# A spectral layer rebuilt as packed real transforms, and a dense layer with one Mish pass

## The chip, the core and the metric

The kernel runs on one core of one Trainium2 chip. The metric is the time that the device takes for one execution, in microseconds (us): 1333.09, the median of three runs between 1329.69 and 1336.48.

## The reference

A sequence of 2048 rows of 1024 bf16 numbers passes through four layers: spectral, dense, spectral, dense. Each normalizes its input and adds its result to that input. Both spectral layers have the same filter, both dense layers the same weights.

```python
def _A_ref(x, w_r, w_i):                      # spectral
    B, S, D = x.shape                         # 1, 2048, 1024
    X = jnp.fft.rfft2(x.astype(jnp.float32), axes=(-2, -1))
    X = X * (w_r + 1j * w_i)                  # (2048, 513)
    return jnp.fft.irfft2(X, s=(S, D), axes=(-2, -1)).astype(jnp.bfloat16)

def _B_ref(x, w1, b1, w2):                    # dense, F = 3584
    h = jnp.einsum("bsd,df->bsf", x, w1) + b1
    sp = jnp.log1p(jnp.exp(-jnp.abs(h))) + jnp.where(h > 0, h, jnp.zeros_like(h))
    act = h * jnp.tanh(sp)                    # Mish
    return jnp.einsum("bsf,fd->bsd", act, w2)

x = x + _A_ref(_layernorm(x), A_w_r, A_w_i)
x = x + _B_ref(_layernorm(x), B_w1, B_b1, B_w2)
x = x + _A_ref(_layernorm(x), A_w_r, A_w_i)
x = x + _B_ref(_layernorm(x), B_w1, B_b1, B_w2)
```

## The kernel before

The program has no scheduler: Python code adds instructions to one list per engine (`Prog`), and each list runs in the order in which it was written. `Res` objects remember who wrote and read a buffer last, and `Prog.add` turns that into semaphore waits. So an instruction waits in its engine's queue until its own data are there, and everything behind it on that engine waits too. All DMAs are issued from SyncE's queue (SP, line 247, the noncontiguous one line 246). The residual stream XS (2048 x 1024, bf16) stays in SBUF all the time as 16 tiles of 128 rows; the rest of SBUF is one arena, cut anew in every layer.

`gen_prologue` loads x in four DMAs and takes statistics of the 16 tiles, most of them on VectorE (`tile_stats`), six on ScalarE. `ln_finish` makes scales and offsets for all 16 tiles at once; it needs the statistics of all of them, so a layer starts when the one before has ended.

`gen_layer_A` is the two-dimensional transform as matrix products, one stage after the other over the whole sequence: normalize and transpose (L698), the 1024-point transform along a row as a dense product with the table MD (L722), transposes (L753), 16-point transforms along the sequence (L785, L787), 128-point transforms for each of 16 residues k2 (L819 to L831), the product with the filter on VectorE (L859 to L868), the inverse 128-point transforms (L889 to L901), transposes, inverse 16-point transforms (L934, L936), transposes (L994) and the inverse row transform as a dense product with M5 (L1026), added to XS (L1037). Everything stays in SBUF. MD, M5, the twiddle tables and the filter are loaded in each of the two spectral layers. Evictions from PSUM go through `copy_fn` (L284 on ScalarE, L285 on VectorE).

`gen_layer_B` works on four chunks of 512 rows. `gen_prep` normalizes a chunk (L566) and transposes it (L1196). `gen_mm1` computes h of a chunk, two tiles of 128 features at a time, in 28 groups of 16 matmuls over 8 tiles of the contraction (L1234), with W1 streamed in 28 pieces of 256 columns, hence 14 groups per chunk and 56 loads per layer. VectorE adds the bias (L1240); `emit_act_batch` passes over three groups at a time with Exp (L1127), Ln (L1151) and Tanh (L1158), with table loads between them; `emit_dve_finals` multiplies on GpSimd (L1171). `gen_mm2` multiplies by W2, which is resident (L1275), and adds to XS (L1286). The products of chunk c+1 stand before the output products of chunk c on TensorE.

## Time and profile before

| what | value |
|---|---|
| runs | 1333.09 us median, 1329.69 to 1336.48 |
| profiled execution, span from first to last instruction | 1334.5 us |
| TensorE | 1223.7 us busy, 92% of the span |
| VectorE, ScalarE, GpSimd | 44%, 50%, 18% busy |
| chain that ended last | TensorE 86%, VectorE 7%, ScalarE 4%, DMA 3% |
| read from HBM | 101.31 MB |

The profile has one execution, and its span is its own time; it lies between the runs. A busy share is an average over stages of different kind, and TensorE's busy time counts pipelined matmuls from issue to their modelled end. What a stage costs is read from the windows of that stage, and what a matmul costs in a run of many from the length of the run. A group of instructions shows the mean time of one and how long its engine was idle ahead of it.

### The profile page before, as it was taken

Reading aid. Unit: us, or ns where it says so; the run is one execution under the profiler, and the core shown is the slowest. Engines: PE = TensorE matmul, PEld = TensorE weight load, DVE = VectorE, ACT = ScalarE, POOL = GpSimd, SP = SyncE. Lnnn points to the kernel's source line nnn. Section 1 sums busy time; section 2 is a strip of 40 time slices with the busy share of each in tenths; the row PEclk is TensorE's granted clock in tenths of the full one; section 3 lists DMA queues with packets and bytes.
Section 4 is the critical chain, followed back from the end, with each engine's and each line's share of the span. In section 5 each row is a group of like instructions: output and inputs, shape, how many; then the busy total and the mean of one; then the engine's idle time right before and its main releaser. Section 6 shows DMA issues by size and latency. Waiting matters only on the chain.

```text
span 1334.5 us, 17411 instructions
## 1 busy us (share of the span) xinstructions
PE 1223.7 (92%) x7184; PEld 661.2 (50%) x7184; DVE 591.8 (44%) x1123; ACT 668.6 (50%) x1049; POOL 235.7 (18%) x116
## 2 busy tenths in 40 slices
...
GB/s 268 74 1 40 104 2 1 171 211 123 128 78 10 121 91 0 146 28 0 0 214 1 1 106 38 1 1 292 147 97 153 21 32 158 32 48 189 17 24 24
DMA packets 142958, 106.62 MB, mean 80 GB/s; under 512 B 7200, under 2 KB 130592, under 8 KB 141856
## 3 DMA queue, kind: packets, MB, share of 16 engines
...
q14 instruction: 21, 0.17, 0.0%
HBM read 101.31 MB, written 4.19 MB: 79 GB/s over the span
## 4 chain that ended last, share of the span: by engine, by line
PE 86%; DVE 7%; ACT 4%; DMA 3%; issue 1%; SPq 0%; DVEq 0%
PE PS L1275 29%; PE PS L1234 28%; PE PS L722 8%; PE PS L1026 8%; PE PS L753 2%; DMA ARENA<-in_B_w_dram 2%; DVE ARENA L566 2%; ACT ARENA L284 2%; PE PS L1196 2%; DVE BNST L490 1%; ACT ARENA L569 1%; PE PS L934 1%; PE PS L936 1%; PE PS L787 1%; PE PS L785 1%; DVE ARENA L862 1%
## 5 line engine op out<-in xcount | busy, mean ns | idle before, releaser
L1171 POOL TENSOR_TENSOR ARENA<-ARENA 128x1024 bf16<-128x1024 bf16 x112 | 235.5, 2130 | 1017.1 <-ACT ARENA L1158 1007.5
L1234 PE MATMUL PS<-ARENA 128*128 128x512 bf16 x1792 | 393.6, 382 | 6.0 <-DMA ARENA<-in_B_w_dram 4.4
L1275 PE MATMUL PS<-ARENA 128*128 128x512 bf16 x1792 | 387.8, 379 | 0.0
L1234 PEld LDWEIGHTS PS<-ARENA 128*128 128x128 bf16 x1792 | 176.2, 99 | 219.8 <-issue 11.2
L1275 PEld LDWEIGHTS PS<-ARENA 128*128 128x128 bf16 x1792 | 175.4, 98 | 211.4
L1240 DVE TENSOR_SCALAR ARENA<-PS,B 128x512 bf16<-128x512 f32 x224 | 168.1, 750 | 227.2 <-PE PS L1234 216.7
L1127 ACT ACTIVATE ARENA<-ARENA 128x1024 bf16<-128x1024 bf16 x112 | 112.1, 1044 | 245.3 <-DVE ARENA L1240 245.3
L284 ACT ACTIVATE ARENA<-PS 128x264 bf16<-128x264 f32 (+6 forms) x448 | 152.5, 432 | 118.3 <-PE PS L722 101.0
L1286 DVE TENSOR_TENSOR XS<-PS,XS 128x512 bf16<-128x512 f32 x64 | 44.2, 691 | 322.3 <-PE PS L1275 322.3
L285 DVE CAST ARENA<-PS 128x128 bf16<-128x128 f32 (+3 forms) x244 | 77.8, 365 | 89.3 <-PE PS L722 83.6
L722 PE MATMUL PS<-ARENA 128*128 128x352 bf16 (+1 forms) x768 | 113.2, 310 | 0.0
L1026 PE MATMUL PS<-ARENA 128*128 128x512 bf16 x512 | 110.9, 379 | 0.6 <-DVE ARENA L285 0.6
L1158 ACT ACTIVATE ARENA<-ARENA 128x1024 bf16<-128x1024 bf16 x112 | 110.4, 1046 | 0.4
L1151 ACT ACTIVATE ARENA<-ARENA 128x1024 bf16<-128x1024 bf16 x112 | 110.4, 1046 | 0.4
L285 DVE COPY ARENA<-PS 128x1024 bf16<-128x1024 bf16 (+2 forms) x152 | 78.5, 549 | 49.5 <-PE PS L753 29.5
L548 ACT ACTIVATE STAT<-STAT,EPS 128x16 f32<-128x16 f32 x4 | 1.2, 308 | 196.9 <-DVE STAT L536 194.8
L722 PEld LDWEIGHTS PS<-ARENA 128*128 128x128 bf16 x768 | 75.1, 98 | 37.5
L1026 PEld LDWEIGHTS PS<-ARENA 128*128 128x128 bf16 x512 | 49.9, 98 | 60.9 <-DVE ARENA L285 1.0
L490 DVE BATCH_NORM_STATS2 BNST<-XS 128x6 f32<-128x512 bf16 x116 | 74.2, 681 | 10.5 <-DMA XS<-in_A_x_dram 8.8
L1196 PE MATMUL PS<-IDENT,ARENA 128*128 128x128 bf16 x256 | 28.1, 308 | 39.4 <-DVE ARENA L566 39.4
L698 PE MATMUL PS<-IDENT,ARENA 128*128 128x128 bf16 x256 | 21.9, 250 | 36.2 <-ACT ARENA L569 35.3
L1037 DVE TENSOR_TENSOR XS<-PS,XS 128x512 bf16<-128x512 f32 x64 | 42.6, 665 | 25.6 <-PE PS L1026 25.6
...
## 6 DMA issues: line engine op xcount, KB each, us to landing
ARENA<-in_B_w_dram SPq DMA_DIRECT2D x112, 512.0 KB, 3.8
...
ARENA<-in_A_w_r_dram SPq DMA_DIRECT2D x32, 128.2 KB, 2.5
ARENA<-in_A_w_i_dram SPq DMA_DIRECT2D x32, 128.2 KB, 3.0
...
out_dram<-XS SPq DMA_DIRECT2D x16, 256.0 KB, 3.0
```

What stands on the lines that cost most here:

```text
L284: return lambda e: e.activation(out_ap, in_ap, ACT.Copy)
L285: return lambda e: e.tensor_copy(out_ap, in_ap)
L490: lt = dve.add(lambda e, n2=n2, j=j, lo=lo, hi=hi: e.bn_stats(BNST[:, n2, j, :], XS[:, n2, lo:hi]), waits=w)
L722: e.matmul(PS[:, bank, 0:n], XT[:, db, n2 * P:(n2 + 1) * P], MD[:, db, cs:ce], start=(db == 0), stop=(db == ND - 1)))
L1026: e.matmul(PS[:, bank, 0:n], JT[:, blk, n2 * P:(n2 + 1) * P], M5[:, blk, ds_:de_], start=(blk == 0), stop=(blk == ND - 1)))
L1127: it["tE"] = act.add(lambda e, st=st: e.activation(TMP[st][:, :], HB[st][:, :], ACT.Exp), waits=rT.wait_w() + res_HB[st].wait_r())
L1151: it["tS"] = act.add(lambda e, st=st: e.activation(TMP[st][:, :], TMP[st][:, :], ACT.Ln, bias=1.0, scale=1.0), waits=[(act, it["tE"])])
L1158: it["tT"] = act.add(lambda e, st=st: e.activation(TMP[st][:, :], TMP[st][:, :], ACT.Tanh), waits=[(act, it["tS"])])
L1171: tF = fin.add(lambda e, st=st, dst=dst: e.tensor_tensor(dst, HB[st][:, :], TMP[st][:, :], ALU.mult), waits=w)
L1234: e.matmul(PS[:, bank, 0:SCH], W1B[wslot][:, db, fl * P:(fl + 1) * P], XT[:, db, :], start=(db == 0), stop=(db == ND - 1)))
L1240: e.tensor_scalar(HB[st][:, fl * SCH:(fl + 1) * SCH], PS[:, bank, 0:SCH], B1[:, ft:ft + 1], None, op0=ALU.add),
L1275: e.matmul(PS[:, bank, 0:n], AT[:, ft, j * P:(j + 1) * P], W2[:, ft, ds_:de_], start=(ft == 0), stop=(ft == NF - 1)))
```

## The change

The file is rewritten. Queues, waits and the resident XS stay as they were in kind; the arrangement of rows changes, so that tile j holds rows 128 n2 + 8 j + q (n2 from 0 to 15, q from 0 to 7).

The spectral layer. Each tile is normalized (`ln`, on [128, 1] columns, inverse root by Newton steps on VectorE), written to DRAM (`xn_store`) and read back in another order (`xr_load`), 128 numbers of 256 bytes at a time; both are issued by GpSimd. One product per tile with the 128x128 table M (`s1`) does a 16-point transform along the sequence and an 8-point transform along the row at once, and keeps one real member of each conjugate pair. The 16 residues are then paired in 8 groups; for each group `s2` does the 128-point transforms along the row, `s3` those along the sequence and the filter, `i1` and `i2` the inverses. The groups are pipelined in 12 steps: s2 of group g, s3 of g-1, i1 of g-3, i2 of g-4. In the first spectral layer `filter_bins` also reorders the filter's rows (products with an exchange matrix, copies on GpSimd) and stores the result in DRAM, from where the second reads it. 128 transposes and one product per tile with the transposed table (`i4`) end the inverse; each tile goes to DRAM in 256-byte pieces and comes back in the order of XS (`a_add`), where VectorE adds it and takes statistics and LayerNorm for the dense layer.

The dense layer. The first product of two chunks runs group by group, so that a piece of W1 serves both; a single Mish activation with the bias goes from PSUM to the product's operand. The second half of the sequence is added and normalized between the output products of the first half. In the first dense layer each finished tile is normalized and stored for the next spectral layer, and `s1` of that layer runs between the last output products.

On VectorE, at the start of the program, before:

```order
L268 UNCONDITIONAL_BRANCH [waits barrier_Pool_Activation_PE_DVE_SP_release]
L490 BN_STATS BNST<-XS 128x6 [waits ds_x1]
L490 BN_STATS BNST<-XS 128x6
L492 BN_AGGR STAT<-BNST 128x2 [waits sem_DVE]
L490 BN_STATS BNST<-XS 128x6 x2
```

and now (b1 is the bias of the dense layer, x0 the first tile of x):

```order
L297 UNCONDITIONAL_BRANCH [waits barrier_Pool_Activation_PE_DVE_SP_release]
L375 CAST B1<-B1h 128x28 [waits b1]
L403 BN_STATS ST<-XS 128x6 [waits x0]
L404 BN_STATS ST<-XS 128x6
L405 BN_AGGR ST<-ST 128x2 [waits sem_DVE]
```

The conversion of the bias, which stood in the first dense layer, now stands ahead of the first statistics.

On TensorE, at the start of the first dense layer, before (L1026 ends the spectral layer, L1196 are transposes, L1234 the first product):

```order
L1026 MATMUL PS<-ARENA 128x512 [waits sem_DVE]
L1026 MATMUL PS<-ARENA 128x512 x7
L268 UNCONDITIONAL_BRANCH
L1196 MATMUL PS<-IDENT,ARENA 128x128 [waits sem_DVE]
L1196 MATMUL PS<-IDENT,ARENA 128x128 x31
L1234 MATMUL PS<-ARENA 128x512 [waits ds_w1b0,sem_DVE]
L1234 MATMUL PS<-ARENA 128x512 x15
```

and now, the last of 16 tiles of i4 (L750), transposes of tiles (L793) and the first product (L811):

```order
L750 MATMUL PS<-ARENA,MT 128x512
L793 MATMUL PS<-IDENT,ARENA 128x128 [waits sem_DVE]
L793 MATMUL PS<-IDENT,ARENA 128x128 x7
L793 MATMUL PS<-IDENT,ARENA 128x128 [waits sem_DVE]
L793 MATMUL PS<-IDENT,ARENA 128x128 x7
L793 MATMUL PS<-IDENT,ARENA 128x128 [waits sem_ACT,sem_DVE]
L793 MATMUL PS<-IDENT,ARENA 128x128 x7
L793 MATMUL PS<-IDENT,ARENA 128x128 [waits sem_ACT,sem_DVE]
L793 MATMUL PS<-IDENT,ARENA 128x128 x7
L793 MATMUL PS<-IDENT,ARENA 128x128 [waits sem_ACT,sem_DVE]
L793 MATMUL PS<-IDENT,ARENA 128x128 x7
L811 MATMUL PS<-ARENA 128x512 [waits w1_0,sem_ACT]
```

All 16 tiles of the inverse stand ahead of the first transposes, and the transposes of the second chunk's tiles stand among the first products.

On GpSimd, in the first dense layer, before (its first compute instructions, products of h and the gate):

```order
L1334 MEMSET const-uint8-127 128x1
L268 UNCONDITIONAL_BRANCH [waits barrier_Pool_Activation_PE_DVE_SP_gather]
L1171 ISA
L1171 TENSOR_TENSOR ARENA<-ARENA 128x1024 [waits sem_ACT,sem_DVE]
L1171 TENSOR_TENSOR ARENA<-ARENA 128x1024 [waits sem_ACT] x2
```

and now, among its output products (y_scratch holds the spectral layer's result, xn_scratch the next layer's normalized tiles):

```order
L246 DMA ARENA<-y_scratch 128x1x1024 [waits sem_DVE] x2
L246 DMA xn_scratch<-ARENA 16x8x1024 [waits sem_DVE]
L246 DMA ARENA<-y_scratch 128x1x1024
L246 DMA xn_scratch<-ARENA 16x8x1024 [waits sem_DVE]
L246 DMA ARENA<-y_scratch 128x1x1024
```

Loads of y and stores of the next layer's tiles alternate there. On TensorE at the same place, before:

```order
L1275 MATMUL PS<-ARENA 128x512 [waits ds_w2]
L1275 MATMUL PS<-ARENA 128x512 x83
L1275 MATMUL PS<-ARENA 128x512 [waits sem_DVE]
L1275 MATMUL PS<-ARENA 128x512 x27
L1275 MATMUL PS<-ARENA 128x512 [waits sem_DVE]
```

and now, an output group of 28 products (L828) and the transposes of a later tile (L793) in turn:

```order
L828 MATMUL PS<-ARENA 128x512 [waits w2_2,w2_3,w2_1,w2_0]
L828 MATMUL PS<-ARENA 128x512 x27
L793 MATMUL PS<-IDENT,ARENA 128x128 [waits sem_DVE]
L793 MATMUL PS<-IDENT,ARENA 128x128 x7
L828 MATMUL PS<-ARENA 128x512 x56
L793 MATMUL PS<-IDENT,ARENA 128x128 [waits sem_DVE]
```

Where the output products of a chunk stood alone, eight transposes of a tile that VectorE has normalized now stand after every second group.

The core of the new code:

```diff
+    def prologue(self):
+        sp, dve = self.sp, self.dve
+        xv = self.x[0].rearrange("(n2 j q) d -> j n2 q d", n2=16, j=16)
+        for j in range(16):
+            self.dma(sp, self.XS[:, j, :], xv[j], f"x{j}", writes=[self.r_xs[j]])
...
+        r = Res("b1h")
+        self.dma(sp, self.B1h[:], self.b1.rearrange("(f p) -> p f", p=P), "b1", writes=[r], noncontig=True)
+        self.op(dve, lambda e: e.tensor_copy(self.B1[:], self.B1h[:]), reads=[r], writes=[self.r_b1])
...
+    def ln(self, j):
+        dve = self.dve
+        st, rs = self.ST[:, j, :], self.r_st[j]
+        def on(fn):
+            self.op(dve, fn, reads=[rs], writes=[rs])
+        h, a, r, ri = st[:, 16:17], st[:, 17:18], st[:, 14:15], st[:, 14:15].bitcast(dt.int32)
+        on(lambda e: e.tensor_scalar(h, st[:, 13:14], 0.5, 0.5e-5, op0=ALU.mult, op1=ALU.add))
+        on(lambda e: e.tensor_scalar(ri, h.bitcast(dt.int32), -0.5, float(0x5f3759df - (1 << 22)), op0=ALU.mult, op1=ALU.add))
+        for _ in range(2):
+            on(lambda e: e.scalar_tensor_tensor(a, r, h, r, ALU.mult, ALU.mult))
+            on(lambda e: e.scalar_tensor_tensor(r, a, 1.5, r, ALU.subtract, ALU.mult))
+        on(lambda e: e.scalar_tensor_tensor(st[:, 15:16], st[:, 12:13], -1.0, r, ALU.mult, ALU.mult))
+        b = self.xn_buf[self.xn_n % 3]
+        self.op(dve, lambda e: e.tensor_scalar(b.ap, self.XS[:, j, :], st[:, 14:15], st[:, 15:16], op0=ALU.mult, op1=ALU.add),
+                reads=[self.r_xs[j], rs], writes=[b.res])
+        return b
...
+    def xn_store(self, j, b):
+        self.dma(self.pool, self.xn_d[j].rearrange("q n d -> n q d"), b.ap, f"xw{j % 3}", reads=[b.res],
+                 writes=[self.r_xnd[j]])
+    def xr_load(self, j):
+        k = self.xr_n % 4
+        xr = self.xr_buf[k]
+        self.dma(self.pool, xr.ap, self.xn_d[j].rearrange("q n (h l) -> (n h) q l", l=P), f"xr{k}",
+                 reads=[self.r_xnd[j]], writes=[xr.res])
+        return xr
...
+    def s1(self, j, xr):
+        ps, banks, _ = self.pair()
+        M = self.M
+        fns = []
+        for q in range(8):
+            fns.append(lambda e, q=q: e.matmul(ps[:, q * P:(q + 1) * P], xr.ap[:, q, :], M[:], start=True, stop=True))
+        self.group(fns, reads=[xr.res, self.r_m], writes=banks)
+        src = ps.rearrange("p (q k) -> p k q", q=8)
+        dst = self.Y.ap[:, :, 8 * j:8 * j + 8]
+        if j % 2:
+            self.op(self.act, lambda e: e.activation(dst, src, ACT.Copy), reads=banks, writes=[self.r_y[j]])
+        else:
+            self.op(self.dve, lambda e: e.tensor_copy(dst, src), reads=banks, writes=[self.r_y[j]])
...
+            for j in range(16 + 3):
+                if j < 16:
+                    if j % 2:
+                        self.stats_act(j)
+                    else:
+                        self.stats_dve(j)
+                    self.xn_store(j, self.ln(j))
+                    xr[j] = self.xr_load(j)
+                if j >= 3:
+                    self.s1(j - 3, xr[j - 3])
...
+                for c in range(2):
+                    self.op(pool, lambda e, d3=d3, lo=lo, c=c: e.tensor_copy(d3[:, c, :, 0:64], lo[:, c, 0:3, :]),
+                            reads=[wr[i].res], parts=[wt.res])
+                for kd, c0 in ((0, 7), (1, 3)):
+                    dd = wt.ap[:, :, 384 + 64 * kd:448 + 64 * kd]
+                    self.op(pool, lambda e, dd=dd, lo=lo, c0=c0: e.tensor_copy(dd, lo[:, :, c0, :]),
+                            reads=[wr[i].res], parts=[wt.res])
+                for c in range(2):
+                    src = ps[:, 512 * i + 192 * c:512 * i + 192 * c + 192].rearrange("p (k i) -> p k i", i=64)
+                    self.op(act, lambda e, d3=d3, src=src, c=c: e.activation(d3[:, c, :, 64:128], src, ACT.Copy),
+                            reads=banks, parts=[wt.res])
+                self.dma(sp, self.w_d[s], wt.ap, f"ws{n}", reads=[wt.res], writes=[self.r_wd[s]])
...
+        def s3(g, i):
+            ps, banks, _ = self.pair()
...
+            fns = [
+                lambda e: e.matmul(ps[:, 0:512], t[:, 0:128], z.ap[:, 0, :], start=True, stop=False),
+                lambda e: e.matmul(ps[:, 512:1024], t[:, 0:128], z.ap[:, 1, :], start=True, stop=False),
+                lambda e: e.matmul(ps[:, 512:1024], t[:, 128:256], z.ap[:, 0, :], start=False, stop=True),
+                lambda e: e.matmul(ps[:, 0:512], t[:, 256:384], z.ap[:, 1, :], start=False, stop=True),
+            ]
+            self.group(fns, reads=[z.res, ft.res], writes=banks)
+            x = X[(2 * g + i) % 4]
...
+            wt, yk = WT[(2 * g + i) % 4], YK[(2 * g + i) % 6]
+            ta, tb = T[2 * i], T[2 * i + 1]
+            self.op(dve, lambda e: e.tensor_tensor(ta.ap, x.ap, wt.ap[:, 0:1, :].to_broadcast([P, 2, 512]), ALU.mult),
+                    reads=[x.res, wt.res], writes=[ta.res])
+            self.op(dve, lambda e: e.tensor_tensor(tb.ap, x.ap, wt.ap[:, 1:2, :].to_broadcast([P, 2, 512]), ALU.mult),
+                    reads=[x.res, wt.res], writes=[tb.res])
+            yk.res.begin()
+            self.op(dve, lambda e: e.tensor_tensor(yk.ap[:, 0, :], ta.ap[:, 0, :], tb.ap[:, 1, :], ALU.subtract),
+                    reads=[ta.res, tb.res], parts=[yk.res])
+            self.op(dve, lambda e: e.tensor_tensor(yk.ap[:, 1, :], tb.ap[:, 0, :], ta.ap[:, 1, :], ALU.add),
+                    reads=[ta.res, tb.res], parts=[yk.res])
...
+        for step in range(8 + 4):
+            g2, g3, g4, g5 = step, step - 1, step - 3, step - 4
...
+            for h in range(2):
+                if 0 <= g2 < 8:
+                    s2(g2, h)
+                if 0 <= g2 < 8 and h == 0 and li == 0:
+                    filter_bins(g2)
+                if 0 <= g3 < 8:
+                    s3(g3, h)
+                if 0 <= g4 < 8:
+                    i1(g4, h)
+                if 0 <= g5 < 8:
+                    i2(g5, h)
+            if 0 <= g3 < 8 and g3 + 2 < 8:
+                load_tabs(g3 + 2)
+                load_w(g3 + 2)
+            if 0 <= g4 < 8 and g4 + 2 < 8:
+                load_btabs(g4 + 2)
...
+            for l in range(16):
+                fns.append(lambda e, l=l, m=m, pb=pb: e.transpose(pb[:, l * P:(l + 1) * P], Uall[:, :, 16 * m + l], self.IDENT[:]))
+            self.group(fns, reads=r_u + [self.r_ident], writes=banks)
...
+    def i4(self, j):
...
+        fns = []
+        for h in range(2):
+            fns.append(lambda e, h=h: e.matmul(ps[:, h * 512:(h + 1) * 512], self.MT[:],
+                                               UT.ap[:, 64 * h:64 * h + 64, 8 * j:8 * j + 8], start=True, stop=True))
+        self.group(fns, reads=r_ut + [self.r_mt], writes=banks)
+        sg = self.sg_buf[j % 3]
+        src = ps.rearrange("p (l q) -> p q l", q=8)
+        self.op(self.act, lambda e: e.activation(sg.ap, src, ACT.Copy), reads=banks, writes=[sg.res])
+        self.dma(self.sp, self.y_d[j].rearrange("q n (h l) -> (n h) q l", l=P), sg.ap, f"yw{j % 3}",
+                 reads=[sg.res], writes=[self.r_yd[j]])
+    def a_add(self, j):
+        yt = self.yt_buf[j % 3]
+        self.dma(self.pool, yt.ap, self.y_d[j].rearrange("q n d -> n q d"), f"yr{j % 3}", reads=[self.r_yd[j]], writes=[yt.res])
+        self.op(self.dve, lambda e: e.tensor_tensor(self.XS[:, j, :], self.XS[:, j, :], yt.ap, ALU.add),
+                reads=[yt.res], writes=[self.r_xs[j]])
+        self.stats_dve(j)
+        return self.ln(j)
...
+        def mm1(c, fg):
+            n = base + 14 * (c // 2) + fg
+            wb = self.w1_buf[n % 4]
...
+                at, ra = AT[c % 2], r_at[c % 2][ft]
+                self.op(act, lambda e, bank=bank, ft=ft: e.activation(at.ap[:, ft, :], PS[:, bank, :], ACT.Mish,
+                                                                      bias=self.B1[:, ft:ft + 1]),
+                        reads=[self.r_bank[bank], self.r_b1], writes=[ra])
+            if c % 2 and self.w1_next == n + 4 and n + 4 < base + 28:
+                self.load_w1()
...
+            xs = self.XS[:, j, h * 512:(h + 1) * 512]
+            self.op(dve, lambda e: e.tensor_tensor(xs, PS[:, bank, :], xs, ALU.add),
+                    reads=[self.r_bank[bank]], writes=[self.r_xs[j]])
+            if h == 0:
+                return
+            if last:
+                ov = self.out[0].rearrange("(n2 j q) d -> j n2 q d", n2=16, j=16)
+                self.dma(sp, ov[j], self.XS[:, j, :], "st", reads=[self.r_xs[j]])
+            else:
+                self.stats_dve(j)
+                self.xn_store(j, self.ln(j))
...
+        for j in range(16):
+            self.i4(j)
+        xn = {}
+        for j in range(4):
+            xn[j] = self.a_add(j)
+            if j:
+                transposed(0, j - 1, xn[j - 1], act)
+        transposed(0, 3, xn[3], act)
...
+        for j in range(4, 8):
+            xn[j] = self.a_add(j)
+            if j == 5:
+                mm1(0, 0)
+            elif j == 7:
+                mm1(0, 1)
+            transposed(1, j - 4, xn[j])
+        W2, r_w2 = load_w2()
+        for fg in range(14):
+            if fg + 2 < 14:
+                mm1(0, fg + 2)
+            mm1(1, fg)
+        for t in range(8):
+            xn[8 + t] = self.a_add(8 + t)
+            mm2(t // 4, t % 4, 0)
+            transposed(2 + t // 4, t % 4, xn[8 + t])
+            mm2(t // 4, t % 4, 1)
+        for fg in range(14):
+            mm1(2, fg)
+            mm1(3, fg)
+        for t in range(4):
+            mm2(2, t, 0)
+            mm2(2, t, 1)
+        if not last:
+            self.begin_A()
+            xr = {j: self.xr_load(j) for j in range(4)}
+        j = 0
+        for t in range(4):
+            for h in range(2):
+                mm2(3, t, h)
+                for _ in range(2 if not last and t else 0):
+                    self.s1(j, xr[j])
+                    if j + 4 < 12:
+                        xr[j + 4] = self.xr_load(j + 4)
+                    j += 1
+                if not last and h:
+                    xr[12 + t] = None
+        if not last:
+            while j < 16:
+                if xr.get(j) is None:
+                    xr[j] = self.xr_load(j)
+                self.s1(j, xr[j])
+                j += 1
```

## Rows read from the trace of the kernel before

**Rows 1.** Windows of the four layers: length, busy per engine, PEclk, DMA share, GB/s
```profile
0.00:250.00 250.00, 207.19 (x1672) 140.81 (x1672) 159.46 (x373) 123.83 (x326) 0.20 (x4) 1.00 0.20 65
250.00:676.00 426.00, 403.76 (x1920) 189.00 (x1920) 153.51 (x228) 219.25 (x212) 117.75 (x56) 0.97 0.29 87
676.00:906.00 230.00, 209.82 (x1672) 142.79 (x1672) 147.18 (x343) 107.60 (x300) 0.00 (x0) 0.97 0.15 53
906.00:1334.50 428.50, 402.96 (x1920) 188.56 (x1920) 131.63 (x182) 217.96 (x211) 117.75 (x56) 0.97 0.31 96
```

**Rows 2.** Chain of waits in order of time: start us, us, what
```profile
96.59 7.94 PE PS L753 x130
...
260.45 3.64 PE PS L1234 x16
264.10 14.98 DMA ARENA<-in_B_w_dram
...
1035.04 48.35 PE PS L1275 x224
```

**Rows 3.** Groups by line, dense layer: busy us, mean ns, idle before
```profile
L1171 POOL TENSOR_TENSOR ARENA<-ARENA 128x1024 bf16<-128x1024 bf16 x112 | 235.5, 2130 | 1017.1 <-ACT ARENA L1158 1007.5
L1240 DVE TENSOR_SCALAR ARENA<-PS,B 128x512 bf16<-128x512 f32 x224 | 168.1, 750 | 227.2 <-PE PS L1234 216.7
L1151 ACT ACTIVATE ARENA<-ARENA 128x1024 bf16<-128x1024 bf16 x112 | 110.4, 1046 | 0.4
```

**Rows 4.** Groups by shape, ScalarE
```profile
L284 ACT ACTIVATE ARENA<-PS 128x256 bf16<-128x256 f32 x128 | 46.6, 391 | 6.3 <-PE PS L787 6.0
L284 ACT ACTIVATE ARENA<-PS 128x1024 bf16<-128x1024 bf16 x16 | 14.9, 1054 | 0.7 <-PE PS L994 0.7
```

**Rows 5.** Timeline of SyncE's queue: start us, us, engine, line, operation
```profile
35.20 0.45 SPq L247 DMA_DIRECT2D ARENA<-in_A_w_i_dram  x1
```

**Rows 6.** Window of the first 40 us
```profile
0.00:40.00 40.00, 10.70 (x133) 8.94 (x134) 27.17 (x65) 27.32 (x37) 0.20 (x4) 1.00 0.76 281
```

**Rows 7.** DMA issues: count, KB each, median us to landing
```profile
ARENA<-in_B_w_dram SPq DMA_DIRECT2D x112, 512.0 KB, 3.8
ARENA<-in_A_w_r_dram SPq DMA_DIRECT2D x32, 128.2 KB, 2.5
out_dram<-XS SPq DMA_DIRECT2D x16, 256.0 KB, 3.0
B1h<-in_B_b_dram SPq DMA_DIRECT2D x1, 7.0 KB, 10.1
```

**Rows 8.** Timeline of VectorE, statistics and small operations
```profile
23.15 0.17 DVE L539 TENSOR_SCALAR STAT<-STAT 128x12 f32<-128x12 f32 x1
23.34 0.17 DVE L540 TENSOR_TENSOR STAT<-STAT 128x6 f32<-128x6 f32 x1
...
250.24 1.29 DVE L490 BATCH_NORM_STATS2 BNST<-XS 128x6 f32<-128x512 bf16 x2
251.56 0.21 DVE L492 BATCH_NORM_AGGREGATE STAT<-BNST 128x2 f32<-128x12 f32 x1
```

**Rows 9.** Groups by shape, VectorE
```profile
L566 DVE TENSOR_SCALAR ARENA<-XS,STAT 128x1024 bf16<-128x1024 bf16 x48 | 32.8, 749 | 0.1
L859 DVE TENSOR_TENSOR ARENA<-ARENA 128x1040 bf16<-128x1040 bf16 x32 | 22.2, 693 | 5.0 <-ACT ARENA L847 5.0
L866 DVE TENSOR_TENSOR ARENA<-ARENA 128x520 bf16<-128x520 bf16 x32 | 13.7, 429 | 1.1
L285 DVE COPY ARENA<-PS 128x1024 bf16<-128x1024 bf16 x80 | 53.3, 687 | 18.6 <-PE PS L1196 12.2 <-PE PS L698 3.3 <-PE PS L994 2.5
L1286 DVE TENSOR_TENSOR XS<-PS,XS 128x512 bf16<-128x512 f32 x64 | 44.2, 691 | 322.3 <-PE PS L1275 322.3
```

**Rows 10.** Windows after waits of TensorE, first dense layer
```profile
266.70:270.30 3.60, 3.56 (x33) 3.50 (x34) 2.07 (x3) 0.00 (x0) 0.00 (x0) 0.53 1.05 387
279.20:283.60 4.40, 4.38 (x13) 1.67 (x14) 0.75 (x1) 4.37 (x5) 0.00 (x0) 0.63 0.37 97
```

1665 lines of the change are left out of this document (524 added, 1141 removed).

## The prediction

> **What bounds the kernel now.** I read the windows by stage first, then the chain of waits, then the groups. Before, the four layers take 250, 426, 230 and 428.5 us [rows 1]; TensorE is busy in 207, 404, 210 and 403 us of them, and the chain runs through it almost everywhere. A run of 224 dense matmuls takes 48.35 us, 0.216 us each [rows 2]. A dense layer has 1792 of these: 387 us that the change keeps. So each dense layer has some 39 us to win, half of it at its start: 16 matmuls, then 15 us of waiting for weights [rows 2]. The spectral layers, 480 us together, have everything else. ScalarE's three passes, VectorE's bias and GpSimd's product in the dense layer [rows 3] all lie beside TensorE; what they free is no gain by itself.
>
> **Dense arithmetic.** Removed per layer: three ACTIVATEs of 1.05 us for each of 56 groups, their table loads, 112 bias adds of 0.75 us, 56 products of 2.1 us. Added: 112 Mish passes over 128x512 out of PSUM. No row shows Mish; from below the 0.39 us of 128x256 [rows 4], from above all three old passes on half a tile, 3 x 1.05 / 2 = 1.6 us. Both are under the 1.73 us (8 x 0.216) that TensorE needs per group, so it costs 0 at either end. W1 is loaded 28 times a layer instead of 56; the loads lay under matmuls already: 0.
>
> **First spectral layer.** (a) VectorE's first instruction now waits for the b1 load, which stands behind 22 other issues on SP. An issue takes 0.45 us [rows 5], so b1 goes out at about 11 us; 5.7 MB stand ahead of it, at 281 GB/s [rows 6] 20 us; b1 itself took 10.1 us from issue to landing [rows 7], less what overlaps. I take 29 us, between 21 and 31. (b) A LayerNorm tile on VectorE costs 1.53 us of statistics, 7 small dependent operations spaced 0.2 us [rows 8] and a 0.75 us scaling [rows 9]: 3.7 us. (c) Each of 16 tiles then goes through DRAM on GpSimd's queue, where the load back stands behind the landing of its own store and ahead of the next store. The trace before has no DMA issued by GpSimd. A 256 KB store took 3.0 us from issue to landing [rows 7]; issuing the load, in 1024 pieces of 256 bytes, lies between one SP issue, 0.45 us, and the whole 3.8 us of a W1 load, also of 1024 pieces [rows 7]. A round is thus 3.45 to 6.8 us; I take 5.0, near the middle because neither row is nearer. VectorE needs about 3.7 plus half an eviction per tile, so GpSimd is the later one. 29 + 3.7 + 16 x 5.0 + last load 3.8 + 8 cold matmuls 0.9 [rows 10] + eviction 1.05 [rows 4] = 118.5 us until the packed stages may start.
> (d) Packed stages, per residue group: TensorE has 52 matmuls of 256 columns or their equal (16 x 256, 8 x 512, 16 x 256, 12 x 256 + 4 x 512), at half of 0.216 us per 256 columns 7.4 us. ScalarE has six evictions of 1.05 us, 6.3 us. VectorE has two filters, each 2 x 0.69 + 2 x 0.43 [rows 9], and about four 512-column evictions of 0.75 [rows 3]: 7.5 us. I take 7.8 us for each of the four steps in which all stages run; the filling steps come to 3.5, 5, 5.5 and 6 us by the same counts, the draining ones to 6, 4, 4 and 3.5, a cold start to 1.5: 70 us. In the first layer a loop through the filter adds to that: load landed, 12 matmuls (1.0), GpSimd's 8 copies (2.7, by elements from 2.1 us for 1024; 17 us if a copy costs as much as that product), 7 SP issues (3.2), next load landed (3.0): 9.9 us a step. With two steps of 5 us, whose loads come early, six of 9.9 and 17.5 us of draining it is 87 us; 70 is the lower end, and 17 us a copy would add 85. (e) 128 transposes at 7.94/130 us [rows 2] with evictions of 2 x 0.69 us, 9 us. First layer: 118.5 + 87 + 9 = 214.5 us, against 250.
>
> **Dense layer start.** (f) The last inverse stage is 16 tiles through DRAM again: eviction, SP store in 256-byte pieces, GpSimd load, add, statistics, LayerNorm (4.4 us a tile on VectorE). The first dense transposes stand behind all 16 tiles on TensorE, and tile 15 cannot start before store 9 has landed, as three staging tiles rotate. A store of 1024 pieces: b1's 3584 pieces in 10.1 us give 2.9 us, W1's 3.8 is the upper end, three in flight without a limit (5.3 us / 3) 1.8 the lower. With 2.9 (the row of small pieces), TensorE is free of the tiles 33 us after the transposes, then goes tile by tile behind VectorE, and steady matmuls begin at 56 us (49 to 64), 32 of 896 matmuls being done by then. Lower and upper end of the start come from 1.8 and 3.8 in the same steps. (g) The rest of the layer is 387 - 7 us of matmuls and the other 64 transposes, 4 us: 56 + 380 + 4 = 440 us where nothing else waits. The last layer ends with an eviction, an issue and a store, 4 us more: 444, against 428.5. W2, 7.3 MB, stands on SP behind the 16 stores; 26 us at 281 GB/s, and wanted only after two chunks of the first product, 97 us: 0, and so is W1 behind it. The 15 us that the start of the old layer lost to W2 ahead of W1 [rows 2] go with that, but the start loses more, as said.
>
> **A new wait in the first dense layer.** (h) Its second half is normalized between the output matmuls of its first half, tile by tile. GpSimd's queue there holds: load y of tile 8+t, store of the next layer's tile t, load y of 9+t. That store waits for LayerNorm of tile t, after the second output group of t. So after that group's end: eviction 0.69, LayerNorm 3.7, two issues 0.9, landing 3.0, then add and LayerNorm 4.4: 12.7 us until the transposes of 9+t may run. TensorE has only one output group of 28 x 0.216 = 6.05 us to cover it: it stands 6.7 us, seven times (t = 1 to 7). With 2.5 us to land [rows 7] and free issues it is 5.3; with GpSimd issues of 3.8 us, 13. After a wait the trace before shows transposes at a granted clock of 0.53 (the 1.2 GHz level), and 13 dense matmuls at 0.63 in 4.38 us instead of 2.8 [rows 10]; so each restart costs 2.0 us more. 7 x 8.7 = 61 us: 501 us, against 426. The last layer has no such stores and no such wait.
>
> **Second spectral layer.** (i) Its first transform runs between the last output groups; exposed stay LayerNorm and eviction 4.4, store 3.5, load 4.3, stage 2: 14 us, 17 with issues at 1.55 us. 17 + 70 + 9 = 96 us, against 230.
>
> **Sum.** 214.5 + 501 + 96 + 444 = 1255 us, against 250 + 426 + 230 + 428.5 = 1334.5, the profiled execution, which lies 1.4 us above the median 1333.09 of the runs. So 1254 us.
>
> **Rivals.** R1, GpSimd's queue decides: issuing a 1024-piece load keeps it far longer than SP. At 5.1 us per issue the rounds of (c) cost 16 x 3.55 = 57 us more, and the second layer's 16 loads no longer hide under 48 us of output groups, some 22 more: level with before. At 6.5 us: 79 + 43, 1376 us. Against it: SP's 0.45 us; for it: no row shows this queue. The Trainium skill (DMA: Bandwidth & Descriptors, SWDGE vs HWDGE vs iDMA) says that such a DMA's descriptors are computed by software on GpSimd's cores; no run here shows it yet. By the same page (Anatomy of one DMA) the store would be 2.0 us plus bytes at 436 GB/s, an estimate of 2.6 us, and the sum 6 us less.
> R2, the wait of (h) is not there, because the pieces land sooner or TensorE has other work, and GpSimd's rounds go at 3.45 us: 1254 - 61 - 25 = 1168 us. For it only that no row prices this queue; against it the order of the three engines.
> R3, 256-byte stores to DRAM go at half the speed, 5.8 us each: tile 15 waits 26 us longer in both dense layers, 1306 us. b1's 2-byte pieces, 2.8 ns each, show no such doubling, but go to SBUF. The Trainium skill (DMA: Bandwidth & Descriptors, Specifications) says that below 512 bytes the engine reads, modifies and writes, which speaks against this change; by it the sum would be 1306.
> That the change does not do what it says is excluded by the order: Mish stands once per group, W1 28 times a layer.
>
> **Chances.** Forecast (1195 to 1300) 0.62, R2 0.12, R3 0.08, R1 0.16, the rest, 0.02, near level. Range 1150 to 1350: R2's cheap ends below (filter loop at 7.8, b1 at 21), R1 at 6 us above. Half a per cent is about what a measurement of this kernel tells from no change. Faster 0.80 (forecast, R2, R3 less 0.02), same 0.04, slower 0.16.
>
> **What would show it.** VectorE idle until about 29 us; GpSimd rounds of 5 us; steps of 10, later 8 us; TensorE waiting for VectorE's L423 seven times by 6 to 7 us in the first dense layer, none of it in the last; 90 to 100 us from the first dense layer's end to the second spectral one's last transpose. Wrong it would be by GpSimd's issue time, or if (h) is not found.

## The result, and the profile after

The changed kernel takes 1273.2 us (median of four runs, 1272.35 to 1273.78) against 1332.9 beside it: a ratio of 0.9553, interval 0.9535 to 0.9571. The forecast was 1254 us and a gain: the gain and the range of 1150 to 1350 us hold, and the time lies 19 us above the forecast.

The windows of the four layers of the changed kernel, which answer to [rows 1]: length, then busy time of TensorE, its weight loads, VectorE, ScalarE and GpSimd, granted clock, DMA share, GB/s.

```profile
0.00:218.40 218.40, 109.50 (x801) 84.61 (x802) 123.58 (x278) 94.79 (x124) 55.84 (x100) 0.97 0.45 128
218.40:733.00 514.60, 435.55 (x2032) 197.67 (x2032) 146.25 (x406) 103.07 (x138) 27.04 (x43) 0.91 0.26 73
733.00:833.50 100.50, 81.23 (x624) 62.47 (x624) 74.66 (x108) 61.90 (x54) 4.06 (x5) 0.94 0.28 87
833.50:1270.10 436.60, 414.27 (x1952) 187.73 (x1952) 91.60 (x236) 96.44 (x132) 8.35 (x16) 0.96 0.27 75
```

The second spectral layer gave 129.5 us and the first 31.6; the dense layers took 88.6 and 8.1 back, 97 of 161 us. In part that is work that has moved, since the second spectral layer's first stage (L459) now runs in the first dense layer; the larger part, as the next rows show, is new waiting and the low clock behind it. TensorE was 92% busy before and is 82% busy now.

Three stretches inside the first dense layer, same columns: the second half's normalization between output groups, the products of its second half, and its last output groups.

```profile
357.30:525.60 168.30, 115.91 (x514) 52.49 (x512) 65.73 (x184) 0.69 (x1) 7.42 (x14) 0.82 0.09 25
525.60:622.30 96.70, 96.70 (x450) 43.87 (x448) 3.96 (x12) 37.79 (x55) 0.55 (x1) 1.00 0.26 74
622.30:733.00 110.70, 103.44 (x529) 48.42 (x526) 38.92 (x98) 5.80 (x6) 14.37 (x19) 0.98 0.19 50
```

Each stretch has 448 dense products. The middle one takes 96.7 us, 0.216 us a product as in [rows 2], with Mish passes and W1 loads beside it; the first is 71.6 us longer: 52.4 us of waiting, 11.6 us of slower products and 7.7 us of transposes. What it waits for is one line of the waits (us in all, times, longest):

```profile
PE PS L793 <- DVE ARENA L423: 52.4, 7, 7.6
```

One of these seven waits, in the chain of waits (start us, us, what; the small VectorE steps left out):

```profile
363.81 6.06 PE PS L828 x28
...
369.96 0.70 DVE XS L833
370.69 0.69 DVE ST L403
...
373.72 0.56 DVE ARENA L423
...
374.56 0.53 POOL xn_scratch L246
375.10 3.83 DMA ARENA<-y_scratch
378.95 0.70 DVE XS L763
...
382.71 0.56 DVE ARENA L423
...
383.32 1.04 PE PS L793 x8
384.35 8.17 PE PS L828 x28
```

From the end of the output group at 369.87: addition and LayerNorm of tile t, GpSimd's store for the next layer, only then the load of y(9+t), its addition and LayerNorm, the transposes. TensorE meanwhile has one more output group and then stands still from 375.90 to 383.32 us. Its 28 products behind the wait take 8.17 us in place of 6.06. The granted clock from 379.0 us on, and of these products:

```profile
379.00:384.40 5.40, 1.08 (x9) 0.99 (x10) 4.52 (x14) 0.00 (x0) 0.00 (x0) 0.50 0.00 0
384.40:392.50 8.10, 8.10 (x29) 3.26 (x28) 0.68 (x1) 0.00 (x0) 0.00 (x0) 0.75 0.01 2
```

Through the last 4.3 us of the wait and the transposes behind it the clock is 0.50, the 1.2 GHz level, and the products begin at that level.

At the start of the program VectorE's first instruction and two of GpSimd's rounds read (start us, us, instruction, idle before and what ended it):

```profile
25.36 0.18 DVE L375 CAST B<-B1h 128x28 f32<-128x28 bf16 x1 [25.36 <-DMA B1h<-in_B_b_dram]
```

```profile
58.77 0.90 POOL L246 DMA_DIRECT2D ARENA<-xn_scratch  x1 [2.86 <-DMA xn_scratch<-ARENA]
59.67 0.79 POOL L246 DMA_DIRECT2D xn_scratch<-ARENA  x1
63.26 0.90 POOL L246 DMA_DIRECT2D ARENA<-xn_scratch  x1 [2.81 <-DMA xn_scratch<-ARENA]
```

A round (one store, its landing, the load back) takes 4.5 us here, and 4.81 on average: from the first store's issue at 29.32 us to the last load's at 106.24, over 16. Issuing 1024 pieces takes GpSimd 0.90 us, not the 5 us at which the rival R1 would have begun to decide.

Groups by shape (busy us, mean ns of one, idle before), which answer to [rows 3, 4, 9]:

```profile
L815 ACT ACTIVATE ARENA<-PS,B 128x512 bf16<-128x512 f32 x224 | 153.9, 687 | 526.9 <-PE PS L811 526.9
L731 PEld LDWEIGHTS PS<-IDENT,ARENA 128*128 128x128 bf16 x256 | 31.9, 263 | 4.8 <-issue 3.3 <-DVE ARENA L737 1.3
L737 DVE COPY ARENA<-PS 128x2048 bf16<-128x2048 bf16 x10 | 32.3, 3581 | 6.9 <-PE PS L731 6.9
L735 ACT ACTIVATE ARENA<-PS 128x2048 bf16<-128x2048 bf16 x6 | 25.5, 4251 | 12.3 <-PE PS L731 12.2
```

Mish takes 0.69 us, well under TensorE's 1.73 per group, and ScalarE waits for TensorE: the zero in the sum was one. The surprise is the last two lines, the evictions of the 128 transposes (L731): forecast at 1.4 us, they take 3.6 on VectorE and 4.3 on ScalarE.

### The profile page after: what moved, and what is told of

Its sections match the earlier page's. It is cut to its first block, busy times and chain, and to the rows that moved or that the text cites. A ratio compares the mean times of both kernels' runs of the same rounds, so it can differ in the third digit from the quotient of the medians.

```text
span 1270.1 us, 13169 instructions
## 1 busy us (share of the span) xinstructions
PE 1040.5 (82%) x5408; PEld 532.5 (42%) x5408; DVE 436.1 (34%) x1027; ACT 356.2 (28%) x448; POOL 95.3 (8%) x164
## 4 chain that ended last, share of the span: by engine, by line
PE 68%; DVE 14%; DMA 4%; ACT 2%; issue 1%; POOL 0%; SPq 0%; DVEq 0%
PE PS L811 31%; PE PS L828 28%; DMA ARENA<-y_scratch 3%; DVE ARENA L737 2%; DVE ST L403 2%; PE PS L649 1%; PE PS L663 1%; DVE ST L404 1%; PE PS L793 1%; DVE ARENA L423 1%; DVE ST L418 1%; DVE XS L763 1%; PE PS L683 1%; DVE ST L419 1%; DVE XS L833 1%
## 5 line engine op out<-in xcount | busy, mean ns | idle before, releaser
L828 PE MATMUL PS<-ARENA 128*128 128x512 bf16 x1792 | 404.3, 388 | 5.9 <-DVE ARENA L466 4.7
L811 PE MATMUL PS<-ARENA 128*128 128x512 bf16 x1792 | 395.4, 384 | 0.0
L815 ACT ACTIVATE ARENA<-PS,B 128x512 bf16<-128x512 f32 x224 | 153.9, 687 | 526.9 <-PE PS L811 526.9
L828 PEld LDWEIGHTS PS<-ARENA 128*128 128x128 bf16 x1792 | 178.2, 100 | 222.7 <-issue 19.0
L811 PEld LDWEIGHTS PS<-ARENA 128*128 128x128 bf16 x1792 | 177.3, 99 | 215.4 <-issue 9.6
L833 DVE TENSOR_TENSOR XS<-PS,XS 128x512 bf16<-128x512 f32 x64 | 44.2, 691 | 630.2 <-PE PS L828 630.2
L459 PE MATMUL PS<-M,ARENA 128*128 128x128 bf16 x256 | 26.6, 273 | 105.7 <-DMA ARENA<-xn_scratch 96.4
L793 PE MATMUL PS<-IDENT,ARENA 128*128 128x128 bf16 x256 | 25.9, 265 | 72.8 <-DVE ARENA L423 66.6
L464 ACT ACTIVATE ARENA<-PS 128x1024 bf16<-128x1024 f32 x16 | 16.4, 1023 | 197.1 <-PE PS L459 197.1
L459 PEld LDWEIGHTS PS<-M,ARENA 128*128 128x128 bf16 x256 | 20.9, 123 | 112.3 <-DMA ARENA<-xn_scratch 84.1
L793 PEld LDWEIGHTS PS<-IDENT,ARENA 128*128 128x128 bf16 x256 | 20.9, 120 | 82.4 <-DVE ARENA L423 78.3
L750 PE MATMUL PS<-ARENA,MT 128*128 128x512 bf16 x64 | 27.1, 555 | 21.3 <-ACT ARENA L755 17.3
L627 ACT ACTIVATE ARENA<-PS 128x1024 bf16<-128x1024 f32 x32 | 32.9, 1028 | 23.9 <-PE PS L623 23.9
L403 DVE BATCH_NORM_STATS2 ST<-XS 128x6 f32<-128x512 bf16 x56 | 38.8, 693 | 1.6
L404 DVE BATCH_NORM_STATS2 ST<-XS 128x6 f32<-128x512 bf16 x56 | 37.8, 676 | 0.0
L755 ACT ACTIVATE ARENA<-PS 128x1024 bf16<-128x1024 f32 x32 | 31.6, 1023 | 19.7 <-DMA y_scratch<-ARENA 17.4
L423 DVE TENSOR_SCALAR ARENA<-XS,ST 128x1024 bf16<-128x1024 bf16 x64 | 35.1, 548 | 2.4
L731 PE MATMUL PS<-IDENT,ARENA 128*128 128x128 bf16 x256 | 32.7, 290 | 3.4 <-ACT ARENA L691 1.2
L737 DVE COPY ARENA<-PS 128x2048 bf16<-128x2048 bf16 x10 | 32.3, 3581 | 6.9 <-PE PS L731 6.9
```

The source lines that it names most:

```text
L403: self.op(dve, lambda e: e.bn_stats(st[:, 0:6], self.XS[:, j, 0:512]), reads=[self.r_xs[j]], parts=[rs])
L404: self.op(dve, lambda e: e.bn_stats(st[:, 6:12], self.XS[:, j, 512:1024]), reads=[self.r_xs[j]], parts=[rs])
L423: self.op(dve, lambda e: e.tensor_scalar(b.ap, self.XS[:, j, :], st[:, 14:15], st[:, 15:16], op0=ALU.mult, op1=ALU.add), reads=[self.r_xs[ ...
L459: fns.append(lambda e, q=q: e.matmul(ps[:, q * P:(q + 1) * P], xr.ap[:, q, :], M[:], start=True, stop=True))
L737: self.op(dve, lambda e, dst=dst, pb=pb: e.tensor_copy(dst, pb), reads=banks, writes=[r_ut[m]])
L793: fns.append(lambda e, db=db: e.transpose(PSb[:, bank, db * P:(db + 1) * P], xn.ap[:, db * P:(db + 1) * P], self.IDENT[:]))
```

## The experiments

Each was run beside the kernel before on the same chip; "less" is against the changed kernel's 1273.2 us, which stood beside 1332.9 us for the kernel before. Beside the experiments the kernel before took 1331.6 to 1333.1 us, so a difference of a microsecond or two says nothing.

**The bias late.** VectorE's conversion moves from the program's start to the first dense layer's, ahead of i4:

```diff
-        self.op(dve, lambda e: e.tensor_copy(self.B1[:], self.B1h[:]), reads=[r], writes=[self.r_b1])
...
+        if not li:
+            self.op(dve, lambda e: e.tensor_copy(self.B1[:], self.B1h[:]), reads=[self.r_b1h], writes=[self.r_b1])
```

> The conversion of the bias leaves the start of VectorE's queue and stands ahead of the first dense layer's first addition; nothing else changes. Theory: VectorE's first 25.4 us in the changed kernel are the wait for the bias load, and GpSimd's sixteen rounds through DRAM begin behind it, so the rounds start as soon as the first tile of x has landed (6.5 us from issue to landing in the profile, issue at 0.7 us), say at 12 us, and the whole comes out 13 us shorter, 1260 us (1256 to 1265). Rival: the rounds then run beside 5.7 MB of loads, with the DMA engines 90% busy until 40 us, and each early round takes 7 to 9 us in place of 4.65, so that less than 5 us is left: 1268 to 1273.

1265.2 us, 8 less, between the two expectations. GpSimd's first rounds:

```profile
8.19 0.67 POOL L246 DMA_DIRECT2D xn_scratch<-ARENA  x1 [7.74 <-DVE ST L396]
15.94 0.93 POOL L246 DMA_DIRECT2D ARENA<-xn_scratch  x1 [7.08 <-DMA xn_scratch<-ARENA]
16.86 0.55 POOL L246 DMA_DIRECT2D xn_scratch<-ARENA  x1
25.49 0.90 POOL L246 DMA_DIRECT2D ARENA<-xn_scratch  x1 [8.08 <-DMA xn_scratch<-ARENA]
```

They start 21 us earlier, but a store lands 8 us after its issue, beside the loads of the first 40 us, and the last load is issued at 97.1 us in place of 106.2. Of a wait of 25.4 us, 8 were to be had by moving it alone.

**The seven waits, in two steps.** First the load of y(9+t) alone goes ahead of the store; VectorE's order stays:

```diff
+        self.a_load(8)
         for t in range(8):
-            xn[8 + t] = self.a_add(8 + t)
+            xn[8 + t] = self.a_add(8 + t, load=False)
+            if t < 7:
+                self.a_load(9 + t)
             mm2(t // 4, t % 4, 0)
```

> In the second half of the first dense layer the load of y(9+t) is issued one tile earlier on GpSimd, ahead of the store that waits for LayerNorm of tile t; VectorE's order stays. In the changed kernel TensorE waits seven times, 7.5 us each, and runs the next 28 products in 7.0 to 8.2 us in place of 6.05. Theory of the prediction: GpSimd's order (store before load) is one part of the wait, so the 3.9 us from the store's issue to the load's landing go, and seven waits of about 3.5 us remain, which VectorE's own order (addition of tile 9+t behind LayerNorm of tile t) holds: 7 x 3.9 = 27 us less, 1246 us. Rival A: GpSimd's queue is all of it, waits gone: 7 x 9.1 = 64 us less, 1209. Rival B: VectorE's order alone decides and the load was hidden: 1273.

1238.0 us, 35 less. The waits:

```profile
PE PS L797 <- DVE ARENA L423: 18.5, 7, 2.6
```

Seven waits remain, 2.6 us in place of 7.5: VectorE still adds tile 9+t behind LayerNorm of tile t. The theory's 27 us were too few, mainly because each wait lost 4.8 us and not 3.9, 34 us in all; the products and transposes behind them gave some 4 us more, at a granted clock of 0.93 from 358 to 480 us, where the changed kernel's stretch had 0.82. Then the whole step goes ahead:

```diff
+        xn[8] = self.a_add(8)
         for t in range(8):
-            xn[8 + t] = self.a_add(8 + t)
             mm2(t // 4, t % 4, 0)
             transposed(2 + t // 4, t % 4, xn[8 + t])
+            if t < 7:
+                xn[9 + t] = self.a_add(9 + t)
             mm2(t // 4, t % 4, 1)
```

> The whole of the addition, statistics and LayerNorm of tile 9+t, with its load, is written ahead of the second output group of tile t, so that neither GpSimd's queue nor VectorE's holds it behind LayerNorm of tile t. Theory: all seven waits go, and with them the low clock behind them: 7 x (7.5 + 1.6) = 64 us less, 1209 us (1204 to 1216). Rival: VectorE then has 2 LayerNorms of 3.7 us, 2 output additions and a load round in one tile's 12.1 us and becomes late in another place, for one the output group's eviction or the store for the next layer; then half of it stays, 1240 us.

1206.9 us, 66 less (ratio to before 0.9052, 0.9031 to 0.9073). In the chain, TensorE runs through:

```profile
363.21 0.45 PE PS L797 x8
363.66 12.09 PE PS L832 x56
```

So the wait was an order on two engines: GpSimd's queue held a little over half of its cost (35 of 66 us), VectorE's the rest.

**Load j behind store j+1** on GpSimd's queue, in the first layer:

```diff
                     self.xn_store(j, self.ln(j))
-                    xr[j] = self.xr_load(j)
+                if 1 <= j < 17:
+                    xr[j - 1] = self.xr_load(j - 1)
```

> In the first spectral layer the load back of tile j is issued behind the store of tile j+1, so that GpSimd no longer waits for the landing of a store before it issues the next one. Theory: a round of 4.65 us was GpSimd's wait for the landing plus two issues; without the wait VectorE sets the pace, 7.2 us for two tiles with an eviction, 3.6 us each, so 16 x 1.05 = 17 us less, 1256 us. Rival: the transfers themselves are the limit (many small pieces, 1024 each way), rounds stay at 4.3 us or more: 1268 to 1273.

1263.2 us, 10 less. (Of the rival's "1024 each way" only the load is right; a store goes in 128 pieces of 2 KB.) GpSimd now waits for VectorE, as the theory has it, but VectorE takes 8.8 us for two tiles and not 7.2, from one eviction of s1 to the next:

```profile
66.40 1.22 DVE L466 CAST ARENA<-PS 128x1024 bf16<-128x1024 f32 x1
...
72.62 0.21 DVE L394 TENSOR_SCALAR ST<-ST 128x2 f32<-128x2 f32 x1 [1.52 <-ACT ARENA L392]
...
75.18 1.22 DVE L466 CAST ARENA<-PS 128x1024 bf16<-128x1024 f32 x1
```

It waits for ScalarE's statistics of an odd tile, which stand behind an eviction on ScalarE: 1.5 us here, 0.4 us in the pairs between, which take 7.6 us. The wait that was removed uncovered another.

**The evictions of the transposes in halves**, one bank of PSUM each:

```diff
-                self.op(dve, lambda e, dst=dst, pb=pb: e.tensor_copy(dst, pb), reads=banks, writes=[r_ut[m]])
+                for h in range(2):
+                    self.op(dve, lambda e, dst=dst, pb=pb, h=h: e.tensor_copy(dst[:, 1024 * h:1024 * h + 1024], pb[:, 1024 * h:1024 * h + 1024]), reads=banks, parts=[r_ut[m]])
```

> VectorE's evictions of the 128 transposes that end the spectral layer (L737, 2048 elements over two banks of PSUM) are cut in halves of one bank each; ScalarE's stay. In the changed kernel VectorE's take 1.2 to 5.3 us, 3.6 in the mean, five in each layer, and the stage 19.4 us where the prediction had 9. Theory: an eviction over two banks is held up by the transposes that TensorE writes at the same time, one within a bank takes the 0.69 us of such a copy in the kernel before [rows 9]: 8 us less in each layer, 1257 us. Rival: the slowing comes with TensorE's transposes, whatever the eviction's form: two halves of 1.8 us, 1273.

1272.9 us: no gain, the theory falls. **The evictions whole again, transposes of data in one piece.** This kernel leaves out the reordering of the residues, so it shows a cost and is no remedy:

```diff
-                fns.append(lambda e, l=l, m=m, pb=pb: e.transpose(pb[:, l * P:(l + 1) * P], Uall[:, :, 16 * m + l], self.IDENT[:]))
+                fns.append(lambda e, l=l, m=m, pb=pb: e.transpose(pb[:, l * P:(l + 1) * P], Uall[:, 16 * m + l, :], self.IDENT[:]))
```

> Leaves out the reordering of the residues in the last transposes of the spectral layer: each takes 128 numbers that lie one after the other in SBUF, not 128 that lie 256 bytes apart. Number, size and order of all instructions stay. Theory: the wide step of the operand is what slows the evictions beside it (1.2 us alone, up to 5.3) and the transposes themselves (0.127 us each); then the stage falls from 19.4 to some 11 us in each layer, 1257 us. Rival: the step does not matter, 1273.

1254.5 us, 19 less. **The remedy** writes the residues the other way round in i2's eviction:

```diff
-            dst = U[g].ap[:, 8 * half:8 * half + 8, :].rearrange("p a b -> p (a b)")
+            dst = U.ap[:, :, 16 * g + 8 * half:16 * g + 8 * half + 8]
+            ps3 = ps.rearrange("p (k l) -> p l k", l=P)
...
-                fns.append(lambda e, l=l, m=m, pb=pb: e.transpose(pb[:, l * P:(l + 1) * P], Uall[:, :, 16 * m + l], self.IDENT[:]))
+                fns.append(lambda e, l=l, m=m, pb=pb: e.transpose(pb[:, l * P:(l + 1) * P], U.ap[:, 16 * m + l, :], self.IDENT[:]))
```

> The same result as the changed kernel's, with the residues laid down the other way round: the eviction of i2 writes 16 bytes at a time with a step of 256, so that each of the last 128 transposes reads 128 numbers that lie one after the other. The raw filter rows lie in two buffers of W1 until the stage ends, whose two loads come later. Theory: the step of 256 bytes is paid by the transposes and the evictions beside them, and an eviction that writes with such a step costs what it did (as s1's does, 1.02 us on ScalarE and 1.23 on VectorE): 18 us less, 1255 us. Rival: the evictions of i2 take the 0.3 us more each that the transposes save, sixteen per layer, and the packed stage is 5 to 8 us longer: 1262 to 1268.

1257.3 us, 16 less. First the halves, then the remedy, groups by shape (L693 and L694 are i2's evictions, 1.02 and 1.22 us as in the changed kernel):

```profile
L739 DVE COPY ARENA<-PS 128x1024 bf16<-128x1024 bf16 x20 | 32.2, 1844 | 6.8 <-PE PS L731 6.8
```

```profile
L732 PEld LDWEIGHTS PS<-IDENT,ARENA 128*128 128x128 bf16 x256 | 14.3, 98 | 3.3 <-issue 3.3
L738 DVE COPY ARENA<-PS 128x2048 bf16<-128x2048 bf16 x10 | 11.9, 1220 | 6.4 <-PE PS L732 6.4
L736 ACT ACTIVATE ARENA<-PS 128x2048 bf16<-128x2048 bf16 x6 | 11.3, 1877 | 7.4 <-PE PS L732 7.4
L694 DVE CAST ARENA<-PS 128x1024 bf16<-128x1024 f32 x16 | 19.5, 1220 | 9.7 <-PE PS L664 9.7
L693 ACT ACTIVATE ARENA<-PS 128x1024 bf16<-128x1024 f32 x16 | 16.4, 1024 | 6.8 <-PE PS L684 6.8
```

A weight load of 128 numbers takes 98 ns in one piece and 263 with a step of 256 bytes, and the evictions beside it 1.22 and 1.88 us, not 3.6 and 4.3. The stage takes 9.3 us where it took 19. The strided write of i2's evictions costs nothing that shows. The Trainium skill (SBUF — State Buffer, the note on cachelines under Door 1) says that an access which crosses to another 16-byte line each time pays a penalty; the weight load agrees. The same page of the Trainium skill (Who interferes with whom) says that only the pair of ports that VectorE and GpSimd share causes contention; the slow evictions, on VectorE and ScalarE, beside TensorE's strided loads do not fit that. What they wait for inside no trace tells.

**The filter rows one step earlier:**

```diff
-                load_w(g3 + 2)
+                if li:
+                    load_w(g3 + 2)
...
+            if li == 0 and step + 2 < 8:
+                load_w(step + 2)
```

> The filter rows of group s+2 are loaded at the end of step s of the first spectral layer, one step earlier than before. In the changed kernel TensorE waits for these loads at L537 three times, 3.9, 1.5 and 3.2 us, in the third to fifth step, and runs the products behind at half the clock; the later steps of 9.6 us have TensorE busy 97%. Theory from this trace: only those three waits go, 8.6 us and some 2 us of low clock, 1263 us (1260 to 1266). Theory of the prediction: all six steps of 9.9 us are a loop through the filter and fall to 7.8 us: 12 us or more, 1261 at most and no step above 8.5 us. Rival: ScalarE's or GpSimd's copies of the filter come late in place of the loads: 1270.

1266.3 us, 7 less. The filter's products (L537) of the later steps stay 9.3 us apart, where the changed kernel has 9.3 to 9.7:

```profile
138.22 1.55 PE L537 MATMUL PS<-ARENA 128*128 128x64 bf16 x12 [0.22 <-DVE ARENA L612]
147.49 1.55 PE L537 MATMUL PS<-ARENA 128*128 128x64 bf16 x12
156.82 1.55 PE L537 MATMUL PS<-ARENA 128*128 128x64 bf16 x12
```

So only three early steps had been waiting for their filter; in the others TensorE is 97% busy (154 to 183 us of the changed kernel). The loop of the prediction was there in half of its six steps.

**Ten staging tiles:** `sg_buf` has ten buffers in place of three, in the free part of the arena.

> Ten staging tiles in place of three between the last inverse product and the stores to DRAM. In the changed kernel ScalarE waits for the stores 17 us in two layers, and the sixteenth tile leaves TensorE 30.5 us after the first, so the first product of the dense layer, two groups of it, comes behind VectorE's eighth LayerNorm. Theory of the prediction: the three staging tiles set the pace; with ten the tiles leave at 1.03 us each, TensorE is free when tile 3 is normalized, 15 us earlier, and of that the two early groups are worth 5.5 us per dense layer: 1262 us. Rival: the DMA engines set the pace (94% busy between 218 and 267 us), the stores land as late as before and the loads behind them later: 1270 to 1278.

1276.1 us (ratio to before 0.9565, 0.9533 to 0.9598): no gain. TensorE's timeline, first the last tiles of the inverse (L750) in the changed kernel, then here:

```profile
238.65 1.95 PE L750 MATMUL PS<-ARENA,MT 128*128 128x512 bf16 x4 [1.43 <-ACT ARENA L755]
```

```profile
233.14 0.60 PE L750 MATMUL PS<-ARENA,MT 128*128 128x512 bf16 x2 [0.31 <-ACT ARENA L755]
246.93 1.03 PE L793 MATMUL PS<-IDENT,ARENA 128*128 128x128 bf16 x8 [3.18 <-DVE ARENA L423]
262.79 1.03 PE L793 MATMUL PS<-IDENT,ARENA 128*128 128x128 bf16 x8 [5.00 <-DVE ARENA L423]
263.62 5.97 PE L811 MATMUL PS<-ARENA 128*128 128x512 bf16 x16
```

The inverse ends at 233.7 us in place of 240.6, 7 us sooner and not 15: in the changed kernel the sixteenth tile leaves TensorE 22 us after the first begins, not the 30.5 of the theory. The steady products begin no sooner for it. So the staging tiles do not hold the start: the transposes then wait for VectorE's LayerNorm, and the second group of products is written behind the transposes of the third tile of chunk 1. Nor do the DMA engines, busy as they are: VectorE waits for a load of y only ahead of the first tile.

**Rows of 2 KB through DRAM** in place of pieces of 256 bytes, in `xr_load` and in i4's store. This kernel leaves out the reordering and is no remedy either.

> Leaves out the reordering of rows through DRAM: the load back of a normalized tile and the store of an inverse tile move 2 KB per row in one piece, not 256 bytes. Bytes, number and order of the transfers stay. In the changed kernel such a store lands in 2.63 us when alone and 3.5 in the median, such a load in 3.8, a store of 2 KB pieces in 3.3. Theory: pieces of 256 bytes cost little, the landing is mostly latency and load of the engines; stores and loads land at most 0.5 us sooner, a round of GpSimd loses its longer issue (0.90 against 0.54 us), 16 x 0.36 = 6 us, 1267 us (1262 to 1271). Rival, which the prediction had at 8 in 100: stores of 256-byte pieces go at half the speed; then the y stores land in about 1.8 to 2.0 us, sixteen of them leave ScalarE at 1.03 us each, and with the loads 15 us or more go, 1255.

1258.9 us, 14 less, twice the theory and short of the rival. DMA issues, KB each and median us to landing:

```profile
ARENA<-xn_scratch POOLq DMA_DIRECT2D x32, 256.0 KB, 3.1
y_scratch<-ARENA SPq DMA_DIRECT2D x32, 256.0 KB, 2.7
```

In the changed kernel's list these are 3.8 and 3.5. GpSimd's round falls from 4.81 to 4.16 us (30.52 to 97.07 over 16): 0.35 us of the difference is the load's issue, 0.55 against 0.90. A lone store lands in 2.02 us, against 2.63. By the Trainium skill (DMA: Bandwidth & Descriptors, Specifications), under 512 bytes the engine reads, modifies and writes; here a store of 256-byte pieces takes 1.3 times as long. The factor of two was the rival's, and no row shows it.

**Five edits together** (bias late, additions early, load behind store with ScalarE's statistics taken ahead, filter early, residues in one piece):

> Five edits together: the bias late, the additions of the second half one tile earlier, load j behind store j+1 in the first layer (with ScalarE's statistics of a tile taken ahead of its eviction), the filter rows one step earlier, and the residues laid so that the transposes read in one piece. If the five lie in different stages, their gains add: 8 + 66 + 10 to 15 + 7 + 18 = 109 to 114 us, 1159 to 1164 us. Rival: early rounds collide with the loads of the first 40 us, and what a round gives there the next takes back: 1168 to 1175.

1148.9 us, 124 less, where the five gains above add to 107 us. Ten of the 17 us more lie in the rounds: the last load is issued at 76.1 us in place of 106.2, 30 us, where the bias (9.1) and the order (11.2) apart gave 20. ScalarE's statistics taken ahead were not run alone, and two loads of W1, 1 MB, also left the crowded start; what each of these gave is not shown. **And with ten staging tiles and four groups of products ahead:**

```diff
             if j == 5:
                 mm1(0, 0)
-            elif j == 7:
                 mm1(0, 1)
-            transposed(1, j - 4, xn[j])
+                transposed(1, 0, xn[4])
+            elif j == 6:
+                mm1(0, 2)
+                transposed(1, 1, xn[5])
+            elif j == 7:
+                mm1(0, 3)
+                transposed(1, 2, xn[6])
```

> As the five together, with ten staging tiles and with four groups of the first product of chunk 0, not two, before the last transposes of chunk 1. With ten staging tiles alone TensorE was free of the inverse 16 us earlier and nothing came of it, since VectorE's additions and LayerNorms of tiles 4 to 7, 4.9 us each with the copy, ended as late as before, and only two groups of products stood among them. Theory: VectorE sets the start of the dense layer, and two more groups of 16 products, 6.9 us of TensorE's work, now lie beside it in each dense layer: 10 to 14 us less than the five. Rival: the transposes of chunk 1 then wait behind the groups, which wait for W1, and VectorE, which copies them, ends later: no gain.

1138.9 us (1137.4 to 1141.3), 10 less than the five: 0.8537 of the kernel before, interval 0.8515 to 0.8558. TensorE, at the same place as above:

```profile
198.41 9.60 PE L825 MATMUL PS<-ARENA 128*128 128x512 bf16 x32 [1.12 <-ACT ARENA L812]
208.30 3.62 PE L825 MATMUL PS<-ARENA 128*128 128x512 bf16 x16
212.20 3.62 PE L825 MATMUL PS<-ARENA 128*128 128x512 bf16 x16
219.68 7.08 PE L825 MATMUL PS<-ARENA 128*128 128x512 bf16 x32 [0.79 <-DVE ARENA L812]
```

64 products (the first three rows) now lie in the time that VectorE needs, where there were 32. On top of the five the tiles and the groups were not run apart; the tiles alone gave nothing above.

## Why the prediction held, step by step

| step | forecast us | measured us |
|---|---|---|
| (a) VectorE waits for the bias | 29 | 25.4 |
| (c) until the packed stages | 118.5, rounds of 5.0 | 112.3, rounds of 4.81 |
| (d) packed stages, first layer | 87 | 87.1 |
| (e) transposes, each spectral layer | 9 | 19.0 and 18.8 |
| (f) start of a dense layer | 56 | 49.1 in both |
| (h) seven waits with the low clock | 61 | 52.4, 11.6 and 4.1 |
| (i) second layer until its packed stages | 17 | 14.4, and 14.0 in the output groups ahead |
| packed stages, second layer | 70 | 67.3 |

(h) is the step that the order gave away: its place, its number and its chain are in the trace as forecast, and taking it out brought 66 us. The 11.6 are the seven output groups behind the waits, 53.9 us together in place of 42.3; the 4.1 are the transposes ahead of them, at the low clock too. So (h) comes to 68 us.

By layer the forecast was 3.9, 13.6 and 4.5 us short and 7.4 too long. That the whole came so near is in part luck, since errors of some 38 us one way and 24 the other stand against each other:

- (e) was too small by 10 us twice: the evictions were priced by rows without a strided operand beside them, and the transposes too. With the operand in one piece the stage takes 9.3 us, the 9 that were forecast.
- (i) had s1's products between the last output groups free. That stretch has 110.7 us against 96.7, its 80 small products and 4.7 us of waiting for their eviction among them; what stays exposed behind it was 2.6 us less than forecast.
- (h) was too small by 7 us.
- (f) was too large by 7 us twice, at the lower end of its range. The stores overlap: ScalarE takes a new tile every 1.6 us (219.43 to 242.91, over 15), where the forecast had 2.9 for each store, and TensorE is free of the tiles 22 us after the transposes and not 33. With ten staging tiles it is free sooner still and the steady products begin no sooner, so the staging tiles do not set the start; VectorE's eight LayerNorms do.
- (a) and (c) together were too large by 6 us, the packed stages of the second layer by 3.

Of (d) the sum was right and its working half so, which is luck too: three waits of 3.9, 1.5 and 3.2 us, and steps of 9.3 to 9.7 us behind them in which TensorE, with twelve filter products (1.55 us) that the 7.4 us left out, is 97% busy. W1 and Mish cost nothing, as forecast. (The kernel before has 14 groups and 14 pieces of W1 per chunk, not 28: 56 loads per layer, 112 in [rows 7].)

Of the rivals, R1 falls with an issue of 0.90 us and R2 because the wait is there. R3 has the direction right and not the size: a store of 256-byte pieces takes 2.63 us alone and 3.5 in the median, not 5.8, and leaving such pieces out of stores and loads brought 14 us, not 52. GpSimd's own stores landed in 3.3 us in the median, not in the 2.6 of the estimate beside R1.
